# Batch 1's up projection partly in the seven-product form: weight sums from the first down projection on, biases on VectorE, an earlier scale of v, and the second half of first down by block

## The chip, the cores and the metric

The kernel runs on one core of a Trainium2 chip. The metric is the device time of one execution in microseconds (us); three runs of the kernel before lie between 1000.23 and 1001.62, median 1001.16. A core has five engines with queues of their own: TensorE (PE), VectorE (DVE), ScalarE (ACT), GpSimd (POOL) and SyncE (SP), the last for issuing DMAs. Each works through its queue in order.

## The reference

Attention over 8 batches, 8 heads, 576 positions, 64 columns a head, each row looking back over at most 128 positions with a bias that falls with the distance. Then a bilinear feed-forward without a nonlinearity over 4608 tokens:

```
scores = q @ k.T / 8 - slope * |i - j|,  0 <= i - j < 128     (else -1e9)
attn = softmax(scores);  x = attn @ v, heads joined: 4608 x 512
out = ((x @ w_a) * (x @ w_b)) @ w_out        512 -> 1536 -> 512
```

## The kernel before

**Numbers in two halves.** Inputs are float32. Products of the feed-forward run in float16 on pairs (high, low): a high half is a scaled cast, a low half the scaled rest. So every product of two such numbers is three matmuls: high x high, high x low, low x high.

**The up projection, two ways.** A *block* is 128 of the 1536 hidden columns (12 blocks, index `f`), and x of a batch stands in two halves of 288 tokens and two halves of 256 features. `up_plain` (L843) makes a block's a and b for both token halves: 4 sums of 12 matmuls each, `terms` twice per sum. `up_fast` (L858) takes the 2 x 2 split of x and of the weights, with sums of these quarters formed beforehand, and needs 7 sums of 6 matmuls. It reads seven pieces of a block's weights, `wup[:, f, 0:7]`; pieces 3 to 6 are sums of the plain quarters, and forming them overwrites piece 3, which `up_plain` reads. `ways` (L998) says which blocks of a batch go which way; batch 0 is always plain (`first_up`, L781). `halve` (L833) splits the product of a and b into `h`, which the down projection reads.

**The sums of the weights.** `sums_of_weights` (L233) works in 24 units, two for a block. A unit is five GpSimd additions (L246 to L250), a ScalarE cast into the high half (L255) and a VectorE subtraction into the low half (L256), the last two one unit behind the additions. Blocks 0 to 7 use as scratch four places in `wup` of blocks 8 to 11, which hold down weights until those are converted; later blocks use the tile `t` of the scores. The first addition is queued behind the latest bias on GpSimd (`issue_after`), the cast behind the latest main evacuation on ScalarE. `quota` (L1002) deals the units out: 9 and 4 in batch 1's up and down projection, 3 and 5 in batch 2's, 4 in batch 3's down.

**The sums of x.** `split_x` (L440) casts and subtracts quarters of a batch's x into `xs`: four pieces for the plain form, seven for the fast one, eight for both; four GpSimd subtractions (L451 to L461) form the quarters' sums in place, in the buffer of v. It runs while the previous batch's down projection does. The load of the batch after next into that buffer of v (`load_v`, L265) can start only when it has been read for the last time; it stands in SP's queue.

**Attention** (`attention`, L663) runs for batches 1 to 7 as a generator in seven steps for each pair of heads, `i` counting pairs. For a pair: squares and scales of q and k, head layout by four DMAs (L348 to L351), a bias tile (`before_scores`, L359, on GpSimd), scores in four banks (L365), softmax halves `phl`, a DMA transpose to `pT` (L407), then `pv` (L506), the product with v's halves `vhl`. These need v's scale: `v_squares` (L273, ScalarE, sums of squares of each pair) and `v_scale` (L280: a VectorE cast, four small matmuls into `vtot`, three small VectorE instructions in `power_scale`, the last writing `sv`). In every batch the squares are traced in the step of its second pair (p = 1) and the scale in that of its third (p = 2). The first pair's `pv` is done late, at p = 2. `split_v` (L292) has high priority until batch 1 is through.

**What sets the order.** `Pace.along` (L972) puts attention's steps beside a main stream's, `weave` (L954) deals side streams over ranges of its steps. In `first_batch`, batch 0's up projection (49 steps) runs beside the conversion of the weights, and attention as far as 3.2 pairs; its down projection (24 steps) beside the down weights' last conversions and attention to 5.15 pairs. There only SP's order is as written; a scheduler that simulates the timeline orders the other engines by priority and readiness. From batch 1 on TensorE's order is as written, and SP's is not.

**First down** (L809): two token halves; in each, 12 steps over `f` add to four banks at once (four output blocks `e`), 12 matmuls a step; then four evacuations, by VectorE (L825) and ScalarE (L827) in turn, and four DMAs out. There are five banks (`bank`, L59), and two buffers for `row`. Later batches (`down`, L930) go by output block.

Of the kernel before, what the change touches and what calls it, by code (L numbers as in the profile page):

```python
# [23 lines left out]
P = 128  # L24
# [22 lines left out]
def attention_then_bilinear_ffn(ctx: ExitStack, tc: tile.TileContext, qT, kT, vP, w_a, w_b, w_out, rel, slopes2, outT):  # L47
# [185 lines left out]
    def sums_of_weights():  # L233
# [8 lines left out]
        for f, k in [(f, k) for f in range(NF) for k in range(2)] + [(None, None)] * 1:  # L242
            if f is not None:
                a, z = place(), place()
                with tc.issue_after(last_bias[0].ins):
                    pool.tensor_tensor(out=a, in0=wup[:, f, 0:4, 0, k, :], in1=wup[:, f, 0:4, 1, k, :], op=ALU.add)  # L246
# [5 lines left out]
            if len(late) > 1:  # L252
                g, m, x = late.pop(0)
                with tc.issue_after(last_main[0].ins):
                    act.copy(wup[:, g, 3:7, 0, m, :], x)  # L255
                vec.tensor_tensor(out=wup[:, g, 3:7, 1, m, :], in0=x, in1=wup[:, g, 3:7, 0, m, :], op=ALU.subtract)  # L256
# [102 lines left out]
    def before_scores(o, ninv):  # L359
        o.bias = work.tile([P, WIN], F32, tag="bias", name="bias")  # L360
        last_bias[0] = pool.tensor_scalar(out=o.bias, in0=rel_sb, scalar1=ninv, scalar2=sl2_sb[:, o.p:o.p + 1], op0=ALU.mult, op1=ALU.mult)  # L361
# [301 lines left out]
    def attention():  # L663
# [34 lines left out]
        for i in range(n + 1):  # L698
# [9 lines left out]
            if p == 2:  # L708
                v_scale(st)
# [40 lines left out]
            if p == 1:  # L750
                v_squares(st, (0, 1))
            if prev and p == 0:
                states[b - 1] = st
                assert started["down"] == b - 2
                for k, _ in enumerate(split_x(st, b - 1 <= 3, b - 1 >= 2)):
# [5 lines left out]
            if p == 1:  # L761
# [13 lines left out]
    states, started, first_reads, last_read, last_main, last_bias = {}, {"down": -1}, [None], [None], [None], [None]  # L775
# [33 lines left out]
    def first_down(b, oi, h):  # L809

        started["down"] = b
        for t in range(2):
            pss = [bank("dn_ps") for _ in range(NE)]
            for f in range(NF):
                for e in range(NE):
                    for n, (wi, hi) in enumerate(((0, 0), (0, 1), (1, 0))):
                        pe.matmul(pss[e][:, 0:HT], wdn[:, f, wi, e * P:(e + 1) * P], h[:, f, t, hi, :], start=(f == 0 and n == 0), stop=(f == NF - 1 and n == 2))  # L817
                yield

            more = new_hidden()  # L820
            for e in range(NE):
                o = row() if e < 2 else more[:, e - 2, :]
                with tc.high_priority(offset=PRIO):
                    if e % 2:
                        vec.tensor_scalar(out=o, in0=pss[e][:, 0:HT], scalar1=oi, scalar2=None, op0=ALU.mult)  # L825
                    else:
                        act.activation(o, pss[e][:, 0:HT], AF.Copy, scale=oi)  # L827
                act.dma_start(outT[e * P:(e + 1) * P, b * S + t * HT:b * S + (t + 1) * HT], o)
# [237 lines left out]
```

## Time and profile before

| | |
|---|---|
| three runs, us | 1000.23, 1001.16, 1001.62 |
| the profiled execution, us | 1000.39 |
| its span, us | 998.6 |
| mean granted TensorE clock | 0.988 |
| VectorE, ScalarE, GpSimd busy, us | 666.4, 633.7, 257.7 |
| GpSimd on biases (L361), us | 21.4 for 24, and 3.4 for 4 |

Stages by the timeline: attention of batch 0 to 64 us, batch 0's up projection to 165, first down to 211, then batches 1 to 7. A row of the timeline or of the groups gives engine, line and operation, the tiles it writes and reads (out<-in), partitions x elements, a count, and in brackets the idle time before it and what ended that. "PEld" is the weight load that goes with each matmul, so its count is the count of matmuls. Busy time of an instruction includes time in which it is held up after its start.

### The profile page before, as it was taken

Reading aid. Unit: us, or ns where it says so; the run is one execution under the profiler, and the core shown is the slowest. Engines: PE = TensorE matmul, PEld = TensorE weight load, DVE = VectorE, ACT = ScalarE, POOL = GpSimd, SP = SyncE. Lnnn points to the kernel's source line nnn. Section 1 sums busy time; section 2 is a strip of 40 time slices with the busy share of each in tenths; the row PEclk is TensorE's granted clock in tenths of the full one; section 3 lists DMA queues with packets and bytes.
Section 4 is the critical chain, followed back from the end, with each engine's and each line's share of the span. In section 5 each row is a group of like instructions: output and inputs, shape, how many; then the busy total and the mean of one; then the engine's idle time right before and its main releaser. Section 6 shows DMA issues by size and latency. Waiting matters only on the chain.

```text
span 998.6 us, 23815 instructions
## 1 busy us (share of the span) xinstructions
PE 966.7 (97%) x9339; PEld 751.2 (75%) x9339; DVE 666.4 (67%) x1843; ACT 633.7 (63%) x1705; POOL 257.7 (26%) x309
## 2 busy tenths in 40 slices
PE   7899979999999999999999999999999999999998
PEld 5567756777777777777787777777777777877776
DVE  5979999547878566786778677666677576524530
ACT  5967669557766757767767767677666766413321
POOL 1211112113655311452226122131223022211100
PEclk8999979999999999999999999999999999999999
DMA  8435653474345342473533642374334532210001
GB/s 337 163 115 180 225 151 58 108 174 90 77 91 127 112 90 56 90 171 83 106 68 96 167 91 60 80 186 109 72 67 102 161 68 44 49 37 7 1 13 36
DMA packets 148432, 102.82 MB, mean 103 GB/s; under 512 B 120032, under 2 KB 128352, under 8 KB 147296
## 3 DMA queue, kind: packets, MB, share of 16 engines
q1 hardware_dynamic: 138816, 91.77, 37.7%
q10 hardware_dynamic: 9504, 9.54, 3.0%
q8 instruction: 73, 1.20, 0.5%
q14 instruction: 39, 0.32, 0.1%
HBM read 48.33 MB, written 9.44 MB: 58 GB/s over the span
## 4 chain that ended last, share of the span: by engine, by line
PE 72%; DVE 12%; ACT 6%; DMA 6%; issue 2%; SPq 1%; POOL 0%; ACTq 0%; DVEq 0%
PE ch L841 19%; PE dn_ps L937 18%; PE p L841 14%; PE up_ps L841 13%; PE x_ps L503 4%; DMA v<-in_vP 3%; PE sc_ps L380 3%; DVE phl L402 2%; PE dn_ps L817 1%; DVE xs L438 1%; DMA qk<-in_kT 1%; ACT phl L401 1%; ACT t L385 1%; DVE t L384 1%; DVE wup L256 1%
## 5 line engine op out<-in xcount | busy, mean ns | idle before, releaser
L841 PEld LDWEIGHTS <-wup 128*128 128x128 f16 x4224 | 408.3, 98 | 116.7 <-issue 10.5
L937 PE MATMUL dn_ps<-h,wdn 128*128 128x288 f16 x2016 | 254.4, 286 | 0.0
L937 PEld LDWEIGHTS <-wdn 128*128 128x128 f16 x2016 | 193.9, 98 | 51.8
L841 PE MATMUL ch<-xs,wup 128*128 128x288 f16 x1536 | 221.8, 286 | 1.2 <-ACT rc L866 0.7
L841 PE MATMUL up_ps<-xs,wup 128*128 128x288 f16 x1536 | 195.7, 287 | 2.3 <-ACT rc L788 1.5
L841 PE MATMUL p<-xs,wup 128*128 128x288 f16 x1152 | 172.6, 286 | 0.0
L896 POOL TENSOR_TENSOR rc<-rc,row 128x288 f32<-128x288 f32 x64 | 62.1, 971 | 278.0 <-DVE row L894 262.1
L385 ACT ACTIVATE t<-t,mn 128x192 f32<-128x192 f32 (+2 forms) x252 | 107.1, 427 | 25.7 <-DVE mn L384 25.5
L402 DVE SCALAR_TENSOR_TENSOR phl<-t,rin,phl 128x192 f16<-128x192 f32 (+2 forms) x252 | 106.5, 461 | 21.5 <-ACT phl L401 21.3
L834 ACT CAST h<-rc 128x576 f16<-128x576 f32 x96 | 64.1, 668 | 67.0 <-DVE rc L901 37.2
L401 ACT ACTIVATE phl<-t,rin 128x192 f16<-128x192 f32 (+2 forms) x252 | 88.7, 425 | 26.5 <-DMA pT<-phl 13.7
L835 DVE TENSOR_TENSOR h<-rc,h 128x576 f16<-128x576 f32 x90 | 69.1, 768 | 31.5 <-ACT h L834 30.7
L384 DVE CUSTOM_DVE_ANT_0 t<-sc_ps,bias,neg 128x192 f32<-128x192 f32 (+2 forms) x216 | 73.7, 389 | 9.2 <-PE sc_ps L380 9.2
L438 DVE TENSOR_TENSOR xs<-v,xs 128x576 f16<-128x576 f32 x52 | 48.3, 943 | 22.3 <-ACT xs L437 22.1
L942 ACT ACTIVATE row<-dn_ps,oi 128x288 f32<-128x288 f32 x56 | 27.7, 494 | 55.8 <-PE dn_ps L937 55.8
L878 ACT ACTIVATE row<-ch,g 128x288 f32<-128x288 f32 x64 | 31.9, 498 | 48.8 <-PE ch L841 48.8
L873 DVE TENSOR_TENSOR rc<-p,rc 128x288 f32<-128x288 f32 x64 | 29.1, 454 | 44.2 <-PE p L841 34.8
L361 POOL TENSOR_SCALAR bias<-rel_sb,ninv,sl_sb 128x192 f32<-128x192 f32 x24 | 21.4, 891 | 125.9 <-DVE mn L384 125.9
L503 PE MATMUL x_ps<-pT,vhl 128*64 128x128 f16 (+2 forms) x1176 | 44.2, 232 | 8.4 <-ACT vhl L296 5.6
L503 PEld LDWEIGHTS <-vhl 128*64 128x64 f16 x1176 | 41.6, 112 | 13.2 <-ACT vhl L296 5.9
L432 POOL TENSOR_TENSOR xq<-xq,sq 128x576 bf16<-128x576 bf16 x22 | 29.9, 1361 | 72.3 <-ACT sq L431 72.3
L901 DVE SCALAR_TENSOR_TENSOR rc<-rc,g,ch 128x288 f32<-128x288 f32 x64 | 32.6, 510 | 23.6 <-PE ch L841 23.4
(148 smaller groups left out, 1261.9 us busy)
## 6 DMA issues: line engine op xcount, KB each, us to landing
v<-in_vP SPq DMA_DIRECT2D x8, 1280.0 KB, 6.8
out<-row ACTq DMA_DIRECT2D x60, 144.0 KB, 1.8
qk<-in_qT SPq DMA_DIRECT2D x28, 288.0 KB, 4.0
qk<-in_kT SPq DMA_DIRECT2D x28, 288.0 KB, 4.5
wdn<-in_w_a SPq DMA_DIRECT2D x12, 512.0 KB, 5.1
wdn<-in_w_b SPq DMA_DIRECT2D x12, 512.0 KB, 6.0
wdn<-in_w_out SPq DMA_DIRECT2D x12, 512.0 KB, 4.3
qst<-qkh SPq DMA_DIRECT2D x24, 144.0 KB, 2.7
```

The lines of the kernel that those rows point to most:

```text
L384: vec.tensor_tensor_reduce(out=t[:, c:c + w], in0=ps[:, c:c + w], in1=o.bias[:, WIN - w:WIN], scale=-0.125 if o.b == 1 else o.neg, scalar= ...
L385: act.activation(t[:, c:c + w], t[:, c:c + w], AF.Exp, bias=o.mn[:, n:n + 1], scale=-1.0, accum_out=o.sm[:, n:n + 1])
L401: act.activation(phl[:, 0, pc:pc + w], e, AF.Copy, scale=s)
L402: vec.scalar_tensor_tensor(out=phl[:, 1, pc:pc + w], in0=e, scalar=s, in1=phl[:, 0, pc:pc + w], op0=ALU.mult, op1=ALU.subtract)
L438: vec.tensor_tensor(out=xs[:, n, 1, :, :], in0=src, in1=xs[:, n, 0, :, :], op=ALU.subtract)
L503: last = pe.matmul(xp[oc // 512][64 * h:64 * h + 64, o0:o0 + w], vt[0:rows, c:c + 64], probs(pt, rows, blocks, h), start=(n == 0 and first ...
L834: act.copy(h[:, f, :, 0, :], hid)
L835: eng.tensor_tensor(out=h[:, f, :, 1, :], in0=hid, in1=h[:, f, :, 0, :], op=ALU.subtract)
L841: pe.matmul(ps[:, 0:HT], wup[:, a[0], a[1], wi, k, :], xs[:, b, xi, k, :], start=(first and n == 0), stop=(last and n == len(ks) - 1), ski ...
L896: pool.tensor_tensor(out=x0, in0=x0, in1=mid, op=ALU.mult)
L901: vec.scalar_tensor_tensor(out=x1, in0=x1, scalar=st.g, in1=ch, op0=ALU.mult, op1=ALU.mult)
L937: pe.matmul(ps[:, 0:HT], wdn[:, f, wi, e * P:(e + 1) * P], h[:, f, t, hi, :], start=(m == 0 and n == 0), stop=(m == NF - 1 and n == 2))
```

## The change

Six things go together.

- `ways`: batch 1 takes blocks 0 to 3 the fast way and 4 to 11 plain, batches 2 and 3 all twelve fast. `split_x` follows: batch 1's x is split for both ways, later ones for the fast way alone.
- `quota` and `first_batch`: nine units of the weights' sums in steps 12 to 24 of first down, ten in steps 8 to 60 of batch 1's up projection, six in its down projection, none later. The first addition is no longer queued behind a bias.
- The bias is formed by VectorE in place of GpSimd.
- For batch 1 the squares of v are traced one pair earlier (p = 0) and the scale too (p = 1).
- First down's second half goes by output block: for each `e` all twelve `f`, one bank at a time, each emptied before the next but one begins. The first half stays by `f`.
- The evacuations of first down on ScalarE are now what the casts of the weights' sums queue behind.

```
-                with tc.issue_after(last_bias[0].ins):
-                    pool.tensor_tensor(out=a, in0=wup[:, f, 0:4, 0, k, :], in1=wup[:, f, 0:4, 1, k, :], op=ALU.add)
+                pool.tensor_tensor(out=a, in0=wup[:, f, 0:4, 0, k, :], in1=wup[:, f, 0:4, 1, k, :], op=ALU.add)
...
-                with tc.issue_after(last_main[0].ins):
+                with tc.issue_after(last_main[0].ins) if last_main[0] else ExitStack():
...
-        last_bias[0] = pool.tensor_scalar(out=o.bias, in0=rel_sb, scalar1=ninv, scalar2=sl2_sb[:, o.p:o.p + 1], op0=ALU.mult, op1=ALU.mult)
+        vec.tensor_scalar(out=o.bias, in0=rel_sb, scalar1=ninv, scalar2=sl2_sb[:, o.p:o.p + 1], op0=ALU.mult, op1=ALU.mult)
...
-            if p == 2:
+            if p == (1 if b == 1 else 2):
                 v_scale(st)
...
-            if p == 1:
+            if p == (0 if b == 1 else 1):
                 v_squares(st, (0, 1))
...
-                for k, _ in enumerate(split_x(st, b - 1 <= 3, b - 1 >= 2)):
+                for k, _ in enumerate(split_x(st, b - 1 <= 1, b - 1 >= 1)):
...
-            if p == 1:
+            if p == (0 if b == 1 else 1):
                 v_squares(st, (2, 3))
...
+        pss = [bank("dn_ps") for _ in range(NE)]
+        for f in range(NF):
+            for e in range(NE):
+                products(pss[e], f, e, 0)
+            yield
+        more = new_hidden()
+        for e in range(NE):
+            out(pss[e], e, 0, row() if e < 2 else more[:, e - 2, :])
+        for e in range(NE):
+            ps = bank("dn_ps")
             for f in range(NF):
...
+                products(ps, f, e, 1)
+                if f % 4 == 3:
+                    yield
+            out(ps, e, 1, row())
...
-    ways = [(every, [])] * 2 + [(every[6:], every[:6]), (every[10:], every[:10])] + [([], every)] * (B - 4)
+    ways = [(every, []), (every[4:], every[:4])] + [([], every)] * (B - 2)
...
-    quota = [((), ()), (((8, 48, 9),), ((0, 48, 4),)), (((0, 24, 3),), ((0, 48, 5),)), ((), ((0, 48, 4),))] + [((), ())] * (B - 4)
+    quota = [((), ()), (((8, 60, 10),), ((0, 48, 6),))] + [((), ())] * (B - 2)
...
-        weave(att.along(first_down(0, out_scale(st), h), 24, 5.15), (weights, 0, 12, 12))
+        weave(att.along(first_down(0, out_scale(st), h), 24, 5.15), (weights, 0, 12, 12), (spread, 12, 24, 9))
```

`products` holds the three matmuls and `out` the evacuation and the DMA that stood in the loops before; `out` on ScalarE sets `last_main`.

27 lines of the change are left out of this document (11 added, 16 removed).

## The prediction

> **What bounds the kernel now.** I read the page first: the busy shares, the groups, then the span cut into stretches, then TensorE's own timeline with the gaps in it.
>
> ```profile
> span 998.6 us, 23815 instructions
> ...
> PE 966.7 (97%) x9339; PEld 751.2 (75%) x9339; DVE 666.4 (67%) x1843; ACT 633.7 (63%) x1705; POOL 257.7 (26%) x309
> ...
> L841 PEld LDWEIGHTS <-wup 128*128 128x128 f16 x4224 | 408.3, 98 | 116.7 <-issue 10.5
> ...
> L438 DVE TENSOR_TENSOR xs<-v,xs 128x576 f16<-128x576 f32 x52 | 48.3, 943 | 22.3 <-ACT xs L437 22.1
> ...
> L901 DVE SCALAR_TENSOR_TENSOR rc<-rc,g,ch 128x288 f32<-128x288 f32 x64 | 32.6, 510 | 23.6 <-PE ch L841 23.4
> ```
>
> TensorE is busy 97% of the span, so two things can shorten the program: fewer products, or fewer of the 31.9 us (998.6 - 966.7) in which TensorE stands. The stretches show where it stands. Columns: the stretch and its length, then busy us (and instructions) of PE, PEld, DVE, ACT, POOL, then the granted clock, DMA share and GB/s.
>
> ```profile
> 128.00:137.00 9.00, 1.85 (x12) 0.95 (x12) 9.00 (x14) 5.40 (x13) 1.61 (x1) 0.67 0.32 119
> 137.00:146.00 9.00, 8.78 (x83) 6.99 (x84) 7.55 (x16) 5.24 (x13) 0.00 (x0) 0.76 0.62 116
> 146.00:165.00 19.00, 17.82 (x182) 13.07 (x181) 16.82 (x46) 17.56 (x43) 2.49 (x2) 1.00 0.26 41
> 187.00:232.00 45.00, 43.10 (x421) 33.31 (x421) 26.01 (x87) 27.17 (x79) 10.97 (x14) 1.00 0.54 133
> ...
> 240.00:260.00 20.00, 20.00 (x232) 15.83 (x227) 17.62 (x41) 15.42 (x40) 10.63 (x16) 1.00 0.56 113
> ...
> 300.00:320.00 20.00, 19.91 (x214) 15.38 (x211) 17.26 (x40) 13.57 (x35) 12.56 (x12) 1.00 0.44 97
> ```
>
> The one large hole is 128 to 137 us, late in the first batch's up projection: TensorE busy 1.85 of 9.00, VectorE busy for all of it, and the clock at 0.67 there and 0.76 in the 9 us behind it. TensorE's timeline (start, length, line, operands, count, idle time before and what ended it):
>
> ```profile
> 133.57 0.37 PE L503 MATMUL x_ps<-pT,vhl 128*64 128x128 f16 x4 [5.59 <-ACT vhl L296]
> ...
> 137.22 2.61 PE L503 MATMUL x_ps<-pT,vhl 128*64 128x128 f16 x38 [1.80 <-DVE vhl L297]
> 139.76 6.58 PE L841 MATMUL up_ps<-xs,wup 128*128 128x288 f16 x46
> ...
> 192.54 1.51 PE L503 MATMUL x_ps<-pT,vhl 128*64 128x128 f16 x42
> ...
> 210.43 0.19 PE L518 MATMUL n_ps<-xq,ones 128*128 128x64 bf16 x1 [1.37 <-ACT row L827]
> 210.90 1.63 PE L841 MATMUL up_ps<-xs,wup 128*128 128x288 f16 x12 [0.28 <-DVE row L825]
> ...
> 249.72 7.52 PE L841 MATMUL up_ps<-xs,wup 128*128 128x288 f16 x60
> ...
> 321.63 0.18 PE L333 MATMUL qtot<-both,ones 128*128 128x2 bf16 x1 [1.73 <-DVE both L325]
> ```
>
> **Term 1, fewer products.** A plain block of the up projection (12 of them in a batch) has 4 sums of 12 products, 48; a fast one has 7 sums of 6, 42. The plain blocks go from 12, 12, 6, 2 in batches 0 to 3 to 12, 8, 0, 0. The count agrees with the profile: 32 x 48 + 64 x 42 = 4224, the x4224 of the group above; after it is 20 x 48 + 76 x 42 = 4152, 72 fewer. One product costs its place in a full stream: 60 take 7.52 us in the row at 249.72 and 12 take 1.63 at 210.90, so 48 more take 5.89, 122.7 ns each. 72 x 0.1227 = **8.8 us**, all on the engine that bounds batches 1 to 3. A fast block has four VectorE instructions on its sums, each about the 510 ns of L901, where a plain one has two, so VectorE gets 12 x 2 x 0.51 = 12 us more, spread over three of the eight batches; it is busy 67%, and in batches 2 and 3 the weight sums go away, so I put this at nothing. Without that cover it would cost TensorE part of the 12.
>
> **Term 2, the wait for the second batch's scale of v.** This is how the hole comes about:
>
> ```profile
> 119.45 0.25 PE L285 MATMUL vtot<-vc,ones 128*128 128x1 bf16 x4
> ...
> 125.17 0.15 DVE L107 TENSOR_SCALAR cl<-vtot 128x1 f32<-128x1 f32 x1
> ...
> 128.98 0.14 DVE L113 TENSOR_SCALAR r<-cl 128x1 int32<-128x1 int32 x1
> ...
> 132.52 0.14 DVE L114 TENSOR_SCALAR sv<-r 128x1 int32<-128x1 int32 x1
> 132.69 1.55 ACT L296 ACTIVATE vhl<-v,sv 128x640 f16<-128x640 f32 x2 [2.46 <-DVE sv L114]
> ...
> L278 ACT ACTIVATE vsq<-v x4: 720/736/737, 72.5 to 78.1; 128x640 bf16<-128x640 f32 x4
> ```
>
> Three instructions of 0.15 us take from 119.7 to 132.66 because the weight conversions stand between them in VectorE's queue; then ScalarE and VectorE split v, and only then may the products of probabilities and v begin. The squares themselves ran at 72.5 to 78.1 already, so moving them gains nothing by itself; what counts is that the scale (its cast, its four products, its three VectorE instructions) is traced one pair, about 15 steps of the up projection, earlier. 15 steps are at least 15 x 12 x 0.1227 = 22 us, so even behind the same queue it would be there long before it is wanted, and the split with it. What the hole costs: 5.59 + 1.80 of waiting; the 38 products of L503 in 2.61 us where 42 took 1.51 (38/42 of it is 1.37), 1.24 too long; 46 products of L841 in 6.58 where 1.63 + 34 x 0.1227 = 5.80 would do, 0.8 too long. Together **9.4 us**. Not all of it can come back: VectorE has no idle time from 128 to 137, and from 137 to 165 it idles 1.45 + 2.18 = 3.6 us and ScalarE 3.76 + 1.44 = 5.2 us. What is late next is the freeing of the up projection's banks and the first down weights, out of the same full queues. Some of those conversions (twelve VectorE instructions) may slip into the down projection, which reads them one block at a time. The bounds are 0 and 9.4; I take **6**, the 3.6 us of idle time and about a third of the rest.
>
> **Term 3, the second half of first down by block.** Now four banks fill together and are emptied together at the end; TensorE waits 1.37 and 0.28 us at 210. By block, three of the four are emptied beside the next block's 36 products (36 x 0.1227 = 4.4 us), and the up projection goes on in another bank. That gives **1.65 us**. What hides the emptying is those 36 products; if they were not there, the 1.65 stays.
>
> **Term 4, the earlier weight sums.** One unit (a block's half) on GpSimd and VectorE:
>
> ```profile
> L246 POOL TENSOR_TENSOR wup<-wup 128x512 f32<-128x512 f16 x16 | 19.5, 1229 | 0.3
> ...
> L250 POOL TENSOR_TENSOR wup<-wup 128x128 f32<-128x128 f32 x16 | 9.6, 604 | 1.1
> ...
> L248 POOL TENSOR_TENSOR wup<-wup 128x128 f32<-128x128 f32 x16 | 9.1, 571 | 0.0
> ...
> L247 POOL TENSOR_TENSOR wup<-wup 128x128 f32<-128x128 f32 x16 | 8.7, 541 | 31.2 <-DVE wup L256 28.1 <-DVE rin L398 1.8 <-DVE oi L951 1.2
> ...
> L249 POOL TENSOR_TENSOR wup<-wup 128x128 f32<-128x128 f32 x16 | 8.3, 524 | 0.0
> L256 DVE TENSOR_TENSOR wup<-wup 128x512 f16<-128x512 f32 x16 | 14.3, 891 | 5.3 <-ACT wup L255 5.2
> ```
>
> A unit is 1.229 + 0.604 + 0.571 + 0.541 + 0.524 = 3.47 us of GpSimd and 0.89 of VectorE. Nine of them go into the second half of first down: 31 us of GpSimd, 8 us of VectorE. The split of batch 1's x gets four more pieces, 4 x 0.94 = 3.8 us of VectorE, and four more GpSimd subtractions. From 187 to 232 us VectorE was busy 26.0 of 45, GpSimd 11.0; it becomes about 38 and 45. The fast blocks come only at step 32 of batch 1, 32 x 12 x 0.1227 = 47 us after its start, so nobody waits for the sums themselves. The nearest rows to such a load are the stretches 240 to 260 and 300 to 320: VectorE 17.6 and 17.3 of 20, GpSimd 10.6 and 12.6, and TensorE loses 0.00 and 0.09. Right behind the second comes the wait of 1.73. So this costs between nothing and, if VectorE falls behind (below), some 11 us; I take **2**, near the 1.73. A gain is excluded, since no TensorE wait ends on these sums now.
>
> **Term 5, biases on VectorE.** 28 instructions of 128x192 leave GpSimd, where they stood in a queue with the sums, and go to VectorE: between 0.15 (L107 above, two columns) and 0.51 us each (L901, 288 columns, two inputs); I take 0.3, 8.4 us over the whole span, one for each pair. They stand behind the last use of the pair before on the same queue, so they wait for nobody; the next pair's scores wait for them, as now. Hidden by VectorE's idle third: nothing.
>
> Sum: -8.8 - 6 - 1.65 + 2 = -14.45. The profiled execution took 1000.39 us (1.8 us lie outside the span), so 985.9, about **986**. The median of the three runs is 0.8 above the profiled one, far inside the range.
>
> **The rivals.** *The hole only moves.* VectorE and ScalarE are so full from 128 to 165 that TensorE loses behind the missing wait what it lost in it; this also holds the case that the scheduler puts the scale no earlier, as it put the squares where it liked. For it: the 9.00 of 9.00. Against: 3.6 us idle and twelve conversions that may slip. Term 2 is zero: 1000.4 - 8.8 - 1.65 + 2 = 992.
>
> *GpSimd holds up VectorE.* This row pair shows it:
>
> ```profile
> 167.06 2.51 POOL L835 TENSOR_TENSOR h<-rc,h 128x576 f16<-128x576 f32 x2
> ...
> 167.16 1.20 DVE L114 TENSOR_SCALAR sc<-r 128x2 int32<-128x2 int32 x1
> ```
>
> A small instruction of a line that took 0.14 above lasts 1.20 beside one GpSimd instruction of 1.26. The new GpSimd work is 31 us and four subtractions of the same 576 columns, 5 us. If it holds VectorE up for half its length, VectorE needs 38 + 18 = 56 of 45 us and TensorE is 11 late for its banks and scores: 1000.4 - 8.8 - 6 - 1.65 + 11 = 995. If it holds VectorE up for all of it, that is 74 of 45, 29 late, 1000.4 - 16.45 + 29 = 1013. Against both, the second above all: from 240 to 260 the two engines show 17.6 + 10.6 = 28.2 us of work in 20 and TensorE none of it. [...]
>
> *Slower: the loads stand behind the sums.* The next load of v overwrites the buffer that the split of x reads, and the SP queue is in order.
>
> ```profile
> 186.74 0.48 ACT L827 ACTIVATE row<-dn_ps,oi 128x288 f32<-128x288 f32 x1
> ...
> 209.75 0.58 SPq L269 DMA_DIRECT2D v<-in_vP  x1
> ...
> 225.36 0.20 ACT L278 ACTIVATION_READ_ACCUMULATOR vsq<-v 128x1 f32 x1
> ...
> 232.21 0.25 PE L285 MATMUL vtot<-vc,ones 128*128 128x1 bf16 x4
> ```
>
> The first half of first down is emptied from 187 on. If all nine units stand ahead of the split's subtractions on GpSimd, and it is itself slowed by a quarter (39 us), the last read of v comes at 187 + 39 + 5 + 0.9 = 232, the load 22 us later than 209.75, and the head layouts, q and k of the next pair queue behind it. The squares end 6.7 us ahead of the product that needs them, so TensorE waits 15. The hole of term 2 cost 9.4 for 7.4 of waiting, 1.27 times; 15 x 1.27 = 19. The three gains are 16.5 us, so it turns slower from 16.5 / 1.27 = 13 us of waiting, and here it gives 1000.4 - 16.5 + 19 = 1003. Against it: by their place in the program only some four units precede the split, and two of them have room to start before.
>
> **How the numbers follow.** Forecast 0.70, its own range from 1000.4 - 8.8 - 9.4 - 1.65 = 980.5 to 990 (2 of term 2); hole moves 0.15; GpSimd holds up VectorE by half 0.07, by all 0.01; loads behind the sums 0.05; 0.02 for gains and losses that cancel. 0.2% (2 us) is about what a measurement of this kernel can tell from no change. Faster 0.70 + 0.15 + 0.07 = 0.92, same 0.02, slower 0.01 + 0.05 = 0.06. The range 979.5 (a microsecond of the smaller gaps besides) to 994 holds the forecast and the moved hole and leaves out the rest.
>
> **What would show it.** Right: x4152 weight loads at L841's place; vtot before 105 us and no gap of 5.6 us ahead of the first products with vhl; TensorE over 8 of 9 us in that stretch at full clock; no wait on row at the end of first down; batch 1 beginning some 7 us earlier, batch 4 some 14. Wrong: a new gap over 3 us between 150 and 230, ended by bank copies, by scores, or by the load of v; VectorE at 20 of 20 from 187 on.

## The result and the profile after

Seven runs of the changed kernel lie between 1004.36 and 1008.76 us, median 1004.87; seven of the kernel before have the median 1001.16. One of those seven took 1646.30 us and is left out of the ratio, which compares fast runs alone. The ratio is 1.0055 (95% interval 1.004 to 1.007): slower by 3.7 us in the medians and 5.5 by the ratio, where 14 us less were forecast. The profiled execution is the longest of the seven, 1008.76 us, so the stages below together hold up to 3.9 us more than a typical run.

From the page of the changed kernel: span, busy times, the group of the up projection's weight loads.

```profile
span 1007.0 us, 23741 instructions
...
PE 963.3 (96%) x9267; PEld 746.3 (74%) x9267; DVE 692.1 (69%) x1897; ACT 640.3 (64%) x1719; POOL 264.5 (26%) x297
...
L850 PEld LDWEIGHTS <-wup 128*128 128x128 f16 x4152 | 403.2, 98 | 131.5 <-issue 13.9
```

The 72 products are gone (4224 to 4152), yet the time in which TensorE stands has grown from 31.9 to 43.7 us (1007.0 - 963.3). VectorE has 25.7 us more work than before.

The stretches now follow the stages: batch 0's up projection from 64 us, first down, batch 1 up and down, batch 2 up and down. First the kernel before (columns: stretch, length, busy us of PE, PEld, DVE, ACT, POOL, clock, DMA share, GB/s):

```profile
64.00:164.70 100.70, 91.51 (x810) 67.91 (x807) 92.45 (x219) 74.28 (x188) 16.51 (x19) 0.95 0.53 164
164.70:210.90 46.20, 43.52 (x443) 33.20 (x442) 26.72 (x94) 27.13 (x80) 7.72 (x7) 1.00 0.60 130
210.90:292.30 81.40, 80.22 (x797) 63.28 (x797) 59.96 (x163) 57.36 (x157) 37.44 (x52) 1.00 0.46 104
292.30:335.10 42.80, 41.07 (x409) 31.90 (x408) 31.85 (x91) 28.95 (x84) 22.03 (x26) 1.00 0.55 136
335.10:411.00 75.90, 74.92 (x745) 59.15 (x744) 51.53 (x141) 51.41 (x136) 19.53 (x26) 1.00 0.31 66
411.00:452.10 41.10, 40.89 (x408) 31.85 (x406) 30.67 (x92) 28.14 (x81) 20.44 (x25) 1.00 0.66 150
```

And the changed kernel, cut at the same events:

```profile
64.00:164.70 100.70, 90.48 (x802) 66.81 (x802) 95.39 (x223) 75.72 (x190) 19.49 (x23) 0.95 0.52 163
164.70:215.60 50.90, 45.31 (x451) 34.29 (x450) 37.07 (x92) 30.13 (x81) 30.44 (x31) 0.97 0.53 118
215.60:304.30 88.70, 80.90 (x775) 62.43 (x773) 70.69 (x187) 61.47 (x168) 47.96 (x68) 0.96 0.39 88
304.30:350.60 46.30, 42.63 (x408) 32.63 (x407) 37.55 (x105) 32.78 (x95) 30.04 (x37) 0.96 0.62 148
350.60:421.30 70.70, 70.70 (x711) 55.62 (x710) 51.20 (x147) 49.24 (x130) 15.93 (x14) 1.00 0.36 74
421.30:462.00 40.70, 40.70 (x409) 31.91 (x407) 27.41 (x94) 28.88 (x87) 7.08 (x5) 1.00 0.62 157
```

First down begins at 164.7 as before: the hole ahead of it gave nothing back. Then 4.7, 7.3 and 3.5 us are lost in first down and batch 1 (15.5 together), and batch 2 returns 5.6. In the three losing stages the mean clock is 0.96 to 0.97, where it was 1.00 (the last section shows beside which waits).

The hole itself, on TensorE's timeline of the changed kernel:

```profile
125.50 0.41 PE L502 MATMUL x_ps<-pT,vhl 128*64 128x128 f16 x7
...
127.42 1.36 PE L502 MATMUL x_ps<-pT,vhl 128*64 128x128 f16 x35
128.71 0.87 PE L375 MATMUL sc_ps<-qkl,qkh 64*64 64x192 f32 x8
139.67 8.18 PE L850 MATMUL up_ps<-xs,wup 128*128 128x288 f16 x45 [10.09 <-DVE wup L133]
```

The products with vhl run at 125.5 and 127.4 without a wait, as term 2 had it. But right behind them TensorE waits 10.09 us, for something else. VectorE's timeline shows what, in the changed kernel

```profile
102.54 0.14 DVE L114 TENSOR_SCALAR sv<-r 128x1 int32<-128x1 int32 x1
...
138.40 1.21 DVE L133 SCALAR_TENSOR_TENSOR wup<-wdn,wup 128x1024 uint32<-128x1024 uint32 x1
```

and in the kernel before:

```profile
138.49 1.21 DVE L133 SCALAR_TENSOR_TENSOR wup<-wdn,wup 128x1024 uint32<-128x1024 uint32 x1
```

The scale was there 30 us earlier (102.54 for 132.52). But the same instruction, a step in the conversion of the down weights, ended at 139.7 before and 139.6 after, and the tenth block of the up projection waits for it in both; before, the products with vhl had just filled the time up to 139.76. It writes its intermediate into free pieces 4 and 5 of blocks 8 and 9 (`forms[4]`, L87). Block 9's plain pieces 0 to 3 lie between these two places in memory, and the program orders block 9's first product behind the write.

Then the new waits. TensorE's timeline of the changed kernel, some of the rows with a gap:

```profile
194.23 1.54 PE L502 MATMUL x_ps<-pT,vhl 128*64 128x128 f16 x42 [2.04 <-DMA pT<-phl]
208.37 0.41 PE L517 MATMUL n_ps<-xq,ones 128*128 128x512 bf16 x2 [3.12 <-POOL xq L431]
...
232.21 7.96 PE L850 MATMUL up_ps<-xs,wup 128*128 128x288 f16 x50 [2.63 <-DVE rc L863]
...
291.41 0.27 PE L379 MATMUL sc_ps<-qkh,qst 128*64 128x192 f16 x2 [2.33 <-DVE mn L383]
...
335.54 0.18 PE L332 MATMUL qtot<-both,ones 128*128 128x2 bf16 x1 [3.05 <-DVE oi L960]
```

No single one took the place of the hole: they come from GpSimd, VectorE and a transpose, two or three us each. And GpSimd's timeline of the changed kernel shows where the units of the weights' sums went:

```profile
158.27 1.60 POOL L245 TENSOR_TENSOR wup<-wup 128x512 f32<-128x512 f16 x1 [7.35 <-DVE wdn L230]
...
197.11 0.46 POOL L246 TENSOR_TENSOR wup<-wup 128x128 f32<-128x128 f32 x1 [20.30 <-DVE wup L255]
```

The first begin at 158, ahead of first down; then GpSimd stands for 20.30 us behind a VectorE subtraction of a unit, which is itself behind softmax halves, and the additions after it press into the end of first down, between the subtractions of x.

### The profile page after: what moved, and what is told of

The parts are those of the page before. It is cut to its first block, busy times and chain, and to the rows that moved or that the text cites. A ratio compares the mean times of both kernels' runs of the same rounds, so it can differ in the third digit from the quotient of the medians.

```text
span 1007.0 us, 23741 instructions
## 1 busy us (share of the span) xinstructions
PE 963.3 (96%) x9267; PEld 746.3 (74%) x9267; DVE 692.1 (69%) x1897; ACT 640.3 (64%) x1719; POOL 264.5 (26%) x297
## 3 DMA queue, kind: packets, MB, share of 16 engines
q1 hardware_dynamic: 138816, 91.77, 37.1%
## 4 chain that ended last, share of the span: by engine, by line
PE 73%; DVE 9%; DMA 7%; ACT 6%; POOL 2%; issue 2%; SPq 0%; ACTq 0%; DVEq 0%; POOLq 0%
PE ch L850 21%; PE dn_ps L946 17%; PE p L850 15%; PE up_ps L850 10%; PE x_ps L502 4%; DMA pT<-phl 3%; PE sc_ps L379 3%; DMA v<-in_vP 2%; DVE phl L401 2%; ACT t L384 1%; PE sc_ps L375 1%; PE dn_ps L813 1%; DVE xs L437 1%; DMA wdn<-in_w_b 1%; DVE wup L255 1%
## 5 line engine op out<-in xcount | busy, mean ns | idle before, releaser
L850 PEld LDWEIGHTS <-wup 128*128 128x128 f16 x4152 | 403.2, 98 | 131.5 <-issue 13.9
L850 PE MATMUL ch<-xs,wup 128*128 128x288 f16 x1824 | 264.8, 286 | 3.9 <-DVE rc L898 1.8
L850 PE MATMUL p<-xs,wup 128*128 128x288 f16 x1368 | 205.7, 287 | 0.0
L905 POOL TENSOR_TENSOR rc<-rc,row 128x288 f32<-128x288 f32 x76 | 79.1, 1041 | 405.7 <-DVE row L903 363.5
L850 PE MATMUL up_ps<-xs,wup 128*128 128x288 f16 x960 | 126.9, 292 | 14.0 <-DVE wup L133 10.1
L400 ACT ACTIVATE phl<-t,rin 128x192 f16<-128x192 f32 (+2 forms) x252 | 88.7, 425 | 30.7 <-DMA pT<-phl 18.4
L887 ACT ACTIVATE row<-ch,g 128x288 f32<-128x288 f32 x76 | 37.8, 497 | 64.7 <-PE ch L850 64.7
L437 DVE TENSOR_TENSOR xs<-v,xs 128x576 f16<-128x576 f32 x54 | 56.3, 1050 | 17.6 <-ACT xs L436 17.3
L882 DVE TENSOR_TENSOR rc<-p,rc 128x288 f32<-128x288 f32 x76 | 34.5, 454 | 47.6 <-PE p L850 32.1
L910 DVE SCALAR_TENSOR_TENSOR rc<-rc,g,ch 128x288 f32<-128x288 f32 x76 | 38.7, 510 | 24.9 <-PE ch L850 24.9
L384 ACT ACTIVATION_READ_ACCUMULATOR t<-t,mn 128x1 f32 x252 | 47.5, 189 | 0.0
```

The source lines that it names most:

```text
L384: act.activation(t[:, c:c + w], t[:, c:c + w], AF.Exp, bias=o.mn[:, n:n + 1], scale=-1.0, accum_out=o.sm[:, n:n + 1])
L400: act.activation(phl[:, 0, pc:pc + w], e, AF.Copy, scale=s)
L437: vec.tensor_tensor(out=xs[:, n, 1, :, :], in0=src, in1=xs[:, n, 0, :, :], op=ALU.subtract)
L850: pe.matmul(ps[:, 0:HT], wup[:, a[0], a[1], wi, k, :], xs[:, b, xi, k, :], start=(first and n == 0), stop=(last and n == len(ks) - 1), ski ...
L905: pool.tensor_tensor(out=x0, in0=x0, in1=mid, op=ALU.mult)
L910: vec.scalar_tensor_tensor(out=x1, in0=x1, scalar=st.g, in1=ch, op0=ALU.mult, op1=ALU.mult)
```

## The experiments

Two questions: why did the hole not close, and what costs 15 us behind it? For the first, the theory (A) is that the hole had two causes which end at the same moment (the scale of v and the conversion's scratch); the rival is that VectorE and ScalarE are simply full there. For the second, the theories are that the *dealing* of the new work is wrong (B), that *GpSimd's time* is what costs (B1), and that each part of the change has a price of its own on VectorE and attention's chain (C). The runs were taken in four sets, each beside its own runs of the kernel before (medians 1000.9, 1000.84, 1000.06 and 999.6 us), so across sets it is the ratios that are compared. "Own place" is an edit that is not in the change: the last two conversions of down weights write into pieces of `xs` which nothing uses in batch 0.

### The hole: squares alone, own place alone, both, and the change without its sums

Squares alone is the kernel before with the change's fourth point:

```
-            if p == 2:
+            if p == (1 if b == 1 else 2):
                 v_scale(st)
...
-            if p == 1:
+            if p == (0 if b == 1 else 1):
                 v_squares(st, (0, 1))
```

> The kernel before with the earlier squares and scale of v alone. Theory A (the hole of the first up projection has two causes that end at the same moment: the scale of v, and the tenth block's first matmul, which is ordered behind the conversion of the down weights at L133; in the kernel before that conversion ended at 139.70 us and the block began at 139.76, in the changed one 139.61 and 139.67): the wait on vhl goes, a wait of some 8 to 10 us on L133 stands in its place, down projection begins within 1.5 us of 164.7, time within 2 us of before. The forecast's theory (the hole is the scale of v): 3 to 9 us faster.

Measured: 1000.96 us, ratio 1.0002 (0.9988 to 1.0016): nothing. TensorE's timeline:

```profile
138.74 8.77 PE L841 MATMUL up_ps<-xs,wup 128*128 128x288 f16 x49 [9.67 <-DVE wup L133]
```

The wait for vhl is gone and the one for the conversion has taken its whole place.

Own place alone is the kernel before with this edit:

```
+    room = xs[:, 3:7, :, :, :].rearrange("p n a k t -> p (n a k t)").bitcast(F32)
+    own = [room[:, 1024 * n:1024 * n + 1024].rearrange("p (m c) -> p m c", m=2) for n in range(2)]
...
+    def form(n):
+        return own[n - NF - 4] if n >= NF + 4 else forms[n % len(forms)]
...
-        return w[:, :, :, 0], w[:, :, :, 1], forms[n % len(forms)].bitcast(I32)
+        return w[:, :, :, 0], w[:, :, :, 1], form(n).bitcast(I32)
```

> The kernel before, but the last two of the six conversions of down weights write into parts of xs that batch 0 does not use, in place of the free pieces of the weight tile of blocks 8 to 11. Theory A: the wait on the scale of v still holds the products of v at 133 to 137 us, so the time is within 2 us of before. If the dependence on L133 alone had set the hole: 3 to 9 us faster.

Measured: 997.48 us, 0.9967 (0.9955 to 0.998): 3.3 us faster, where the theory of two causes expected no change. First down begins at 155.2, but takes 51.3 us for 46.2. TensorE's timeline:

```profile
123.45 11.08 PE L846 MATMUL up_ps<-xs,wup 128*128 128x288 f16 x89
134.46 0.28 PE L508 MATMUL x_ps<-pT,vhl 128*64 128x128 f16 x4
```

The hole is gone already, from this edit alone: TensorE is busy 12.00 of the 12 us from 128 to 140, for 4.63 before. The scale of v is as late as it was (`sv` at 132.57 for 132.52), and the conversion at 138.5 ends as late too (139.8 for 139.7). But block 9 need not wait for that conversion any more, and the scheduler, which sets TensorE's order in batch 0, put the next blocks' products ahead of those with vhl.

Both edits together:

> Both edits on the kernel before: the earlier scale of v, and the last two conversions into xs. Theory A: with both waits gone the hole of 128 to 140 us closes, 4 to 9 us faster than before, and the first down projection begins at 156 to 161 us. Rival (VectorE is full from 80 to 140 us, so the hole moves to whatever needs VectorE next): no wait over 3 us on L133, but others of the same sum, time within 2 us of before.

Measured: 993.45 us, 0.9932 (0.9918 to 0.9947). TensorE's timeline:

```profile
128.69 3.11 PE L846 MATMUL up_ps<-xs,wup 128*128 128x288 f16 x24
131.73 0.87 PE L381 MATMUL sc_ps<-qkl,qkh 64*64 64x192 f32 x8
132.53 14.14 PE L846 MATMUL up_ps<-xs,wup 128*128 128x288 f16 x114
```

The hole is closed, and first down begins at 151.2 in place of 164.7. By the ratios it is 0.2 us slower for the earlier scale, 3.3 faster for the own place, 6.8 for both. So the theory of two equal causes is half right: the scratch alone made the hole, and the earlier scale is worth nothing while the scratch is in the way, and some 3.5 us once it is not. Of the 13.5 us gained 6.6 are given back in first down and batch 1 up (49.0 and 85.2 us for 46.2 and 81.4). VectorE had worked 92.5 us between 64 us and the start of first down, and now works 83.6, so part of what ran in the hole now runs beside first down.

The change without its sums (`ways`, `quota`, `split_x` and `first_batch` as before):

```
-    ways = [(every, []), (every[4:], every[:4])] + [([], every)] * (B - 2)
+    ways = [(every, [])] * 2 + [(every[6:], every[:6]), (every[10:], every[:10])] + [([], every)] * (B - 4)
...
-        weave(..., (weights, 0, 12, 12), (spread, 12, 24, 9))
+        weave(..., (weights, 0, 12, 12))
```

> The changed kernel with the ways, the dealing of the weight sums and the splitting of x as before: what is left is the biases on VectorE, the earlier scale of v and the second half of first down by block. Theory B (the loss is made by the nine units of sums in first down and the sums and fast blocks in batch 1): 0 to 3 us faster than before, first down 44 to 46 us long and batch 1's up projection 79 to 82. Rival (biases on VectorE or the block order cost it): slower than before by 1 us or more, with first down at 48 or more.

Measured: 1001.27 us, 1.0013 (1.0002 to 1.0025). That is the time of the rival (1 us slower or more), but with first down at 46.8 us and batch 1 up at 83.3, between what the two expected. With the hole open the other parts are worth nothing or a little less, and the sums cost about 4 us more, although they take 72 products out.

### With the hole closed: the change, fewer additions, two other dealings

The change with own place:

> The changed kernel with the last two conversions of down weights in xs (as in the pair of runs that closed the hole on the kernel before). Theory A: the hole closes here too, 5 to 9 us off the changed kernel's 1004.9: 996 to 1000. Rival (GpSimd and VectorE are so loaded behind it that TensorE loses the same time in first down and batch 1): 1002 or more.

Measured: 1005.42 us, 1.0047 (1.0034 to 1.006). First down begins at 155.2, 9.5 us earlier than in the changed kernel, and nothing of it is left at the end, as the rival had it. So with the hole closed the rest of the change costs 11.5 us (1.0047 against 0.9932).

The same with one GpSimd addition for a unit in place of five; the sums of the weights are thereby left out:

```
-                pool.tensor_tensor(out=a, in0=wup[:, f, 0:4, 0, k, :], in1=wup[:, f, 0:4, 1, k, :], op=ALU.add)
-                pool.tensor_tensor(out=z[:, 0, :], in0=a[:, 3, :], in1=a[:, 2, :], op=ALU.add)
...
+                pool.tensor_tensor(out=z, in0=wup[:, f, 0:4, 0, k, :], in1=wup[:, f, 0:4, 1, k, :], op=ALU.add)
```

> The same, but each of the 24 units makes one GpSimd addition (high plus low of the plain pieces) in place of five, so the fast blocks' weights are not the sums; ScalarE's cast and VectorE's subtraction stay. 24 x 2.2 us of GpSimd work go. Theory B1 (GpSimd is what costs: its queue delays the sum of squares of x and the sums of x, and it holds VectorE up): at least 4 us under the run with five additions, and VectorE's instruction at L401 beside it back to 0.45 us. Rival B2 (the casts and subtractions of the units, and the fast blocks, load ScalarE and VectorE in order): within 2 us of it.

Measured: 998.49 us, 0.9977 (0.9965 to 0.9989): 7.0 us less than with all five (1.0047), for some 52 us less of GpSimd work (263.5 to 211.0 over the span).

No units in first down, 9, 8 and 8 in batch 1:

```
-    quota = [((), ()), (((8, 60, 10),), ((0, 48, 6),))] + [((), ())] * (B - 2)
+    quota = [((), ()), (((0, 28, 9), (28, 60, 8)), ((0, 48, 8),))] + [((), ())] * (B - 2)
...
```

> The changed kernel with the conversions in xs, and the nine units dealt to steps 0 to 28 of batch 1's up projection instead of the second half of first down, eight and eight after them. Theory B (the nine units collide with attention and the sums of x in first down): first down 2 to 4 us shorter than with the units in it, at most half of it given back in batch 1: 1 to 4 us under the run with the units in first down. Rival (the load only moves into batch 1): within 1 us.

Measured: 1010.53 us, 1.0098 (1.0085 to 1.0111): 5 us slower than with the change's dealing, which neither expectation had. First down still took 50.4 us, without any unit dealt to it, and batch 1 up 96.3.

Batch 1 plain throughout, the units 12 and 13 in its two projections, batches 2 and 3 fast:

```
-    ways = [(every, []), (every[4:], every[:4])] + [([], every)] * (B - 2)
+    ways = [(every, [])] * 2 + [([], every)] * (B - 2)
...
+    quota = [((), ()), (((8, 48, 12),), ((0, 48, 13),))] + [((), ())] * (B - 2)
...
```

> The changed kernel with the conversions in xs, batch 1 all plain as before, and the sums in batch 1 alone (12 units in its up projection, 13 steps in its down projection); batches 2 and 3 all fast. 48 products fewer than before (5.9 us) instead of 72. Theory B: without sums and sums of x in first down and without fast blocks beside the units nothing of the loss is left but some in batch 1's down projection: 986 to 991. Rival (any denser dealing costs TensorE as much as it saves): 994 or more.

Measured: 1003.74 us, 1.0036 (1.0024 to 1.0048), far from what was expected. Its stretch of batch 1's down projection:

```profile
292.50:340.40 47.90, 42.93 (x408) 32.51 (x407) 39.95 (x99) 33.05 (x91) 40.98 (x53) 0.96 0.47 118
```

GpSimd is busy 40.98 of 47.90 there, and the stage takes 47.9 us where before it took 42.8. Wherever the units are put, the stage that gets them becomes longer; the theory of the dealing (B) fell. (In all four of these runs the additions of the first units ran already from 121 or 122 us on, ahead of first down; below, this is priced by itself.)

### One part each, on the closed hole

Each is squares + own place (993.45 us) with one part of the change. First down's second half by block:

```
+        for e in range(NE):
+            ps = bank("dn_ps")
             for f in range(NF):
...
+                products(ps, f, e, 1)
...
+            out(ps, e, 1, row())
```

> The run with the hole closed (earlier scale of v, conversions in xs; 993.45) plus the second half of first down by block alone. Forecast's term 3: 1.65 us faster than that. Theory C (the stretch from 165 us on is set by VectorE and attention's chain, so a freed bank there is worth nothing): within 1 us of 993.4.

Measured: 995.99 us, 0.9955 (0.9941 to 0.9968): some 2 us slower, little more than the intervals leave open. First down takes 50.1 us for 49.0.

The biases on VectorE, the additions no longer behind one:

```
-                with tc.issue_after(last_bias[0].ins):
-                    pool.tensor_tensor(out=a, ...)
+                pool.tensor_tensor(out=a, ...)
...
-        last_bias[0] = pool.tensor_scalar(out=o.bias, ...)
+        vec.tensor_scalar(out=o.bias, ...)
```

> The run with the hole closed plus the biases on VectorE alone (and the units' first addition no longer behind a bias). Forecast's term 5: within 1 us of 993.4. Theory C (VectorE is the bound to about 230 us): 1 to 4 us slower. Rival D (the unpinned additions of GpSimd, which then start near 158 us beside a full VectorE, make most of the loss): 4 us slower or more.

Measured: 998.36 us, 0.9983 (0.9974 to 0.9991): 5 us slower, the largest price of any part, and what rival D expected. GpSimd's timeline:

```profile
121.32 1.60 POOL L250 TENSOR_TENSOR wup<-wup 128x512 f32<-128x512 f16 x1
...
132.34 1.27 POOL L250 TENSOR_TENSOR wup<-wup 128x512 f32<-128x512 f16 x1
```

The additions of units that are traced for batch 1, after 200 us, run at 121 to 134 us, beside the fullest stretch of VectorE. What had held them back was the bias.

The sums, and casts that queue behind first down's evacuations:

```
+    ways = [(every, []), (every[4:], every[:4])] + [([], every)] * (B - 2)
+    quota = [((), ()), (((8, 60, 10),), ((0, 48, 6),))] + [((), ())] * (B - 2)
...
+                        last_main[0] = act.activation(o, pss[e][:, 0:HT], AF.Copy, scale=oi)
...
+        weave(..., (weights, 0, 12, 12), (spread, 12, 24, 9))
...
```

> The run with the hole closed plus the earlier sums, the fast blocks in batch 1 and twelve fast in batches 2 and 3, and the splitting of x that goes with them; biases stay on GpSimd, first down stays by feature block. Forecast's terms 1 and 4: 8.8 - 2 = 6.8 us faster, 987. Theory C: the 8.8 us come in batches 2 and 3 and are spent before: 993 to 1003, with first down and batch 1's up projection together 8 us or more over the 134.2 us of that run (products removed: 2.9 us of them).

Measured: 995.98 us, 0.995 (0.9937 to 0.9962): 1.8 us slower by the ratios, within what the intervals leave open, for 72 products fewer that were to bring 8.8. Squares + own place, first down and batch 1 up:

```profile
151.20:200.20 49.00, 44.90 (x458) 34.16 (x456) 32.66 (x102) 34.13 (x95) 6.61 (x6) 1.00 0.47 99
200.20:285.40 85.20, 81.75 (x800) 63.94 (x799) 62.80 (x175) 59.65 (x164) 36.68 (x52) 0.98 0.51 115
```

and the same with the sums:

```profile
150.60:203.40 52.80, 44.80 (x459) 34.20 (x458) 39.95 (x106) 36.82 (x100) 23.54 (x26) 1.00 0.45 100
203.40:293.60 90.20, 80.97 (x775) 62.38 (x774) 76.48 (x188) 65.04 (x176) 62.14 (x83) 0.96 0.42 95
```

8.8 us are lost in these two stages, with VectorE at 116.4 of 143.0 us for 95.5 of 134.2; TensorE's work did not grow in them (125.8 us for 126.7).

The changed kernel with own place, the biases back on GpSimd (the second diff above, reversed):

> The changed kernel with conversions in xs (1005.4), the biases back on GpSimd and the units' first addition behind them. Rival D: back to within 3 us of 993.4. Theory C: 1 to 4 us faster than 1005.4, no more, since the sums stay.

Measured: 997.96 us, 0.9977 (0.9967 to 0.9987): 7.0 us less than with the biases on VectorE (1.0047), more than the 1 to 4 of theory C; but it stays 4.5 us above the closed hole (0.9932), where rival D expected less than 3. The parts, each alone on the closed hole, cost 2.3, 5.1 and 1.8 us by the ratios' midpoints, 9.2 together; all of them cost 11.5, a difference that the intervals leave open.

### What of the biases' price is the bias, and other remainders

The biases on VectorE, but the first addition of a unit held behind GpSimd's latest addition for batch squares of x (`xq`):

```
+                with tc.issue_after(last_bias[0].ins):
+                    pool.tensor_tensor(out=a, ...)
...
+            last_bias[0] = pool.tensor_tensor(out=st.xq, in0=st.xq, in1=sq, op=ALU.add)
```

> The run with the hole closed plus the biases on VectorE, with the units' first addition held behind the latest GpSimd addition of x's squares (L432) instead of free. Rival D (the free additions, which started at 121 to 132 us beside a full VectorE, make the loss of about 5 us): within 1.5 us of 993.4. Theory C1 (the bias instructions themselves on VectorE make it): within 1.5 us of the run with free additions, 998.4.

Measured: 994.66 us, 0.9945 (0.993 to 0.996), 3.8 us of the 5.1 back; first down begins at 151.2 again, for 154.2. GpSimd's timeline shows nothing but the splits of h in that time, and idle time between them:

```profile
127.75 1.28 POOL L840 TENSOR_TENSOR h<-rc,h 128x576 f16<-128x576 f32 x1 [6.00 <-ACT h L839]
133.26 1.48 POOL L840 TENSOR_TENSOR h<-rc,h 128x576 f16<-128x576 f32 x1 [4.23 <-ACT h L839]
```

So it is not the 28 instructions on VectorE that cost most (1.3 us are left, within the intervals), but the loss of the hold.

The same hold in the changed kernel:

> The changed kernel with one edit: the units' first addition held behind the latest GpSimd addition of x's squares. Rival D: 2 to 6 us under 1004.9, with no wait of TensorE on xq. Theory C1: within 1 us of it.

Measured: 1004.78 us, 1.0049 (1.0035 to 1.0064): no gain. First down becomes 45.8 us, but batch 1 up 91.0 and down 49.0 (50.9, 88.7 and 46.3 in the changed kernel). The work is only pushed on. There was also less to hold: with the hole open the additions start at 158 (`<-DVE wdn` in the first fence on GpSimd above) and not at 121.

The sums with one addition for a unit, thereby left out again, biases on GpSimd:

```
-                    pool.tensor_tensor(out=a, in0=wup[:, f, 0:4, 0, k, :], in1=wup[:, f, 0:4, 1, k, :], op=ALU.add)
...
+                    pool.tensor_tensor(out=z, in0=wup[:, f, 0:4, 0, k, :], in1=wup[:, f, 0:4, 1, k, :], op=ALU.add)
```

> The run with the hole closed plus the earlier sums and more fast blocks (995.98), each unit with one GpSimd addition in place of five, so the fast blocks' weights are not the sums. Theory B1 (what the sums cost TensorE in first down and batch 1 is GpSimd's time, in its queue and as a hold on VectorE): 988 to 992. Rival B2 (casts, subtractions and fast blocks cost it): 994 or more.

Measured: 995.97 us, 0.9966 (0.9953 to 0.9978), beside 995.98 and 0.995 with all five: no gain. Its two stages:

```profile
150.40:201.80 51.40, 44.66 (x457) 34.10 (x455) 38.85 (x105) 37.73 (x102) 17.15 (x14) 1.00 0.46 102
201.80:292.30 90.50, 81.33 (x776) 62.11 (x775) 71.04 (x189) 62.89 (x172) 31.07 (x25) 0.96 0.43 95
```

GpSimd has little over half the work (48.2 us for 85.7), and the two stages are as long within 1.1 us. GpSimd's time as the general cause (B1) fell; where the additions run free, as in the changed kernel with own place, taking them away gained 7.0 us. By elimination the price of the sums lies with the casts and subtractions, the fast blocks and the doubled split of x, on ScalarE and VectorE; no run parts these.

A milder version: squares + own place, seven blocks of batch 2 fast and all of batch 3, 18 products fewer:

```
...
+    ways = [(every, [])] * 2 + [(every[7:], every[:7])] + [([], every)] * (B - 3)
+    quota = [((), ()), (((8, 48, 9),), ((0, 48, 6),)), (((0, 20, 3),), ((0, 48, 7),))] + [((), ())] * (B - 3)
```

> The run with the hole closed and a little of the change: batch 2 takes seven blocks fast, batch 3 all twelve (18 products fewer, 2.2 us), units dealt 9, 6, 3, 7 over the up and down projections of batches 1 and 2, none in first down. Theory B (only the dealing into first down and beside batch 1's fast blocks loses): 990 to 992.5, faster than all so far. Rival (any denser dealing costs as much as it saves): 993 to 996.

Measured: 993.73 us, 0.9936 (0.9922 to 0.9951): nothing over 993.45, where 18 x 0.1227 = 2.2 us were there to be had; the intervals leave a gain of up to 1.7 us open. The version that beats both kernels most stays squares + own place.

## Why the prediction was wrong, point by point

By the ratios the forecast was 20 us off: 14.45 faster forecast, 5.5 slower measured. The change without its sums (terms 2, 3 and 5) was to gain 7.65 us and lost 1.3; the sums and the fast blocks (terms 1 and 4) were to gain 6.8 and lost 4.2. Two steps failed, the cause of the hole in term 2 and the size of term 4.

**What bounds it.** That the hole at 128 to 137 us was the place of the loss was right. That its cause was the row with the wait of 5.59 on vhl was not: with the scratch of two conversions moved and vhl as late as before, TensorE did not stand there.

**Term 2 failed first** (6 forecast, 0 shown by squares alone: the wait for the scale of v went, and one of 9.67 us for the conversion stood in its place). Its step "what is late next is the freeing of the up projection's banks and the first down weights" named what is late, but not that it was already late at the same moment: the block at 139.76 in the prediction's own fence began 0.06 us after the conversion of 138.49 ended, and it waited for that conversion's scratch. The trace named one releaser for each gap; whoever was second, by a hair, was not in it. That some conversions could slip was taken as room, but this one held block 9. The rival "the hole only moves" was right on this term, with another mechanism than full engines: with own place the same conversions stand in the same queues, and the hole closed.

**Term 1 was right, in its place.** Batches 2 and 3, up and down, went from 231.0 to 222.7 us in the profiles (75.9 + 41.1 + 72.2 + 41.8 and 70.7 + 40.7 + 70.6 + 40.7), 8.3 for the 5.9 of their 48 products and the unit work that left them. The other 24 products, in batch 1, bought nothing: its up projection got 7.3 us longer. So the 122.7 ns of a product were had where TensorE hardly waits (batches 2 and 3), and not in batch 1.

**Term 4 was mis-sized** (2 forecast, bounds 0 to 11). First down and batch 1 lost 15.5 us in the profile, some of it term 5's and 24 products notwithstanding; on the closed hole the sums alone lost 8.8 us in first down and batch 1 up. If the 72 products count with their full 8.8 us, the sums cost 4.2 + 8.8 = 13.0 us on the open hole and 1.8 + 8.8 = 10.6 on the closed one. Its step "The nearest rows to such a load are the stretches 240 to 260 and 300 to 320", where "TensorE loses 0.00 and 0.09", failed: those stretches did not show what the same load does in first down. The reason is argued, not shown: first down stands on attention's chain (scores, softmax, transpose, products with v, sums of squares for the next scale), and when VectorE is late so is the chain, although the busy shares show room (37.1 of 50.9).

**GpSimd holds up VectorE** was given 0.07 at 995, and it is part of it. VectorE's timeline before, and then after:

```profile
200.81 1.46 DVE L402 SCALAR_TENSOR_TENSOR phl<-t,rin,phl 128x192 f16<-128x192 f32 x4 [0.52 <-ACT phl L401]
```

```profile
208.52 1.90 DVE L401 SCALAR_TENSOR_TENSOR phl<-t,rin,phl 128x192 f16<-128x192 f32 x2 [0.82 <-ACT phl L400]
```

Four such instructions took 1.46 us, and now two take 1.90 (the row ends with its window; all four take 3.66). Counted over all VectorE instructions that overlap one of GpSimd from 165 to 216 us, each against the tenth percentile of its own kind, the lengthening grew from 2.9 to 11.9 us while GpSimd's work grew by 22.7 (7.72 to 30.44); in the changed kernel the 41 that overlap none are 0.2 us longer in all. That is 0.4 us for each us that GpSimd works more (9.0 / 22.7), nearer to a hold for half of its length than for all of it. The same count from 118 to 151 us on the closed hole gives 7.6 us where the additions run free beside batch 0's up projection and 4.0 where they are held, and there first down begins at 154.2 and 151.2. But fewer additions took off 7.0 us in one setting and nothing in the other, so it does not carry the rest.

**Term 3** (1.65 forecast) had its mechanism right: no wait on row is left at the end of first down. On the closed hole it made the program some 2 us slower all the same, at the edge of what the intervals tell. That the banks were late because attention was, so that TensorE now waits for attention, is only argued, and why it would be worse and not equal was not settled.

**Term 5** (nothing forecast) was sized by its 28 instructions, and these do cost little: 1.3 us, within the intervals. But the edit also took away the hold on the additions, 3.8 us on the closed hole, to which the prediction gave no price. In the changed kernel itself that hold is worth nothing (1.0049 for 1.0055), as its additions start only at 158. Two readings of terms 4 and 5 were off without weight: the row of L107 has one column, not two, and 11 + 31 + 5 us of GpSimd are 47, not 45.

**The slower rival**, loads behind the sums, was not what happened: 1003 was near the result, but no gap of 15 us ahead of the next scale is there; the nearest are 3.12 at 208 and 2.63 at 232.

What stays open: which link of attention's chain makes first down last 49 to 53 us once the hole is closed, where it takes 46 with the hole, and which of the casts, the subtractions, the fast blocks and the split of x makes the price of the sums.

## What to carry to other kernels

Where a wait is to be removed, look for the second instruction that ends at the same moment: delete the first releaser in thought, and follow the waiting instruction's other inputs, the places that they were written to included, for scratch in the holes of a tile can order work that shares no data (in the changed kernel TensorE waited 10.09 us for the write of 138.40). Before a gain in a stage where TensorE does not wait is paid for in another, measure that other stage under the load: busy shares of another stage did not tell it here. And when an operation moves to another engine, price the orderings that hung on it, not its instructions alone (here, on the closed hole, 3.8 of 5.1 us).

## What the runs showed of the hardware

Behind some waits of TensorE the clock was lower, behind others it was not. The changed kernel in slices of 4 us, around its waits of 2.04 (from 192 on) and 3.12 us (ending at 208.37):

```profile
192.00:196.00 4.00, 1.96 (x51) 1.71 (x46) 1.50 (x9) 1.88 (x6) 0.00 (x0) 1.00 0.18 58
196.00:200.00 4.00, 4.00 (x38) 2.98 (x37) 3.91 (x8) 3.72 (x9) 2.81 (x4) 1.00 0.10 37
...
204.00:208.00 4.00, 1.25 (x11) 0.87 (x9) 2.38 (x9) 1.76 (x6) 4.00 (x5) 1.00 0.76 184
208.00:212.00 4.00, 3.63 (x21) 2.45 (x21) 3.48 (x4) 3.75 (x8) 4.00 (x6) 0.71 0.12 39
212.00:216.00 4.00, 4.00 (x43) 2.85 (x42) 4.00 (x6) 1.75 (x4) 4.00 (x5) 0.87 0.83 175
216.00:220.00 4.00, 4.00 (x35) 3.21 (x34) 3.93 (x15) 1.39 (x6) 3.29 (x6) 1.00 0.98 178
```

Behind 2.04 us the clock stays at 1.00; behind 3.12 us it is 0.71 and 0.87 for 8 us, by an estimate 4 x 0.29 + 4 x 0.13 = 1.7 us more. The products agree: 24 of first down took 4.77 us from 208.61, where 24 took 3.11 from 195.70. Behind the waits of 2.63 (at 232) and 2.33 us (at 291) it fell likewise, to 0.69 and 0.63 in a slice. Behind 2.72 us in the closed-hole kernel with the sums (at 193) it stayed at 1.00, so in these runs the length of the wait alone does not tell where the clock falls. The wait at 208 and the slower products behind it make 3.12 + 1.7 us together. Batch 1's down projection lost 3.5 us, 1.94 in idle time (42.80 - 41.07 = 1.73 before, 46.30 - 42.63 = 3.67 after) and 1.56 in slower products.
